# Decoding and splitting weights 1,024 columns at a time in an attention, Fourier and feed-forward kernel, with a new order of all its steps

## The chip, the cores and the metric

The kernel runs on one NeuronCore of a Trainium2 chip. The time is device microseconds of one execution, from its first to its last instruction and what the device puts around them; several runs are made, and their median counts.

## What is computed

The reference, cut to what matters:

```python
# q, k, v: (8 batches, 8 heads, 576 tokens, 64), float32
rel = pos[:, None] - pos[None, :]
mask_local = (rel >= 0) & (rel < 32)                       # heads 0 to 3
mask_strided = (rel >= 0) & (pos[None, :] % 32 == pos[:, None] % 32)   # heads 4 to 7
attn = softmax(where(mask, q @ k.T / 8, -1e9)) @ v
x = attn.transpose(0, 2, 1, 3).reshape(8, 576, 512)
mixed = real(fft(fft(x, axis=1), axis=2))
u = x + mixed
un = (u - mean(u)) / sqrt(var(u) + 1e-6)                   # over the 512 channels
out = u + maximum(un @ w_ch1, 0) @ w_ch2                   # w_ch1 512x2048, w_ch2 2048x512
```

All work is in float32 accuracy. Long matrix products are made of three float16 products: each operand is split into a high and a low half.

## The kernel before

**Weights.** They arrive as words of 64 bits, in 16 pieces of 128 partitions by 512 columns for each of W1 and W2, and each piece is decoded on the chip (`weights`, L1143). SP loads the piece into a borrowed buffer (L1156). ScalarE scales its high words (c1), ScalarE (L1165) or VectorE (L1167) shifts its low words right, VectorE combines the two (c2, L1171), and later VectorE puts the sign back (c3, L1177). Behind c2 four small matmuls (`gram_piece`, L1207) add the piece's squares in a PSUM bank; from four pieces of W1 (`quarter`), or all sixteen of W2 (`weights2`, L1251), come a norm (L1226 to L1228) and a power-of-two scale (L375 to L378). With it W1's pieces are split into halves (`split`: ScalarE L1247, VectorE L1249). W2's are split by `scaled` (ScalarE L1283, VectorE L1285, and SP copies the high half into its place, L1287). W1 is decoded into the memory that W2's result needs later, so a piece of W2 is combined only when the piece of W1 in its place has been split. While a Gram bank is open and TensorE would wait, matmuls on zeros (fillers, `rest`, L1215) are put in.

**Where the pieces land.** `S0` and `S1` in the table `P` name the buffer that each late piece borrows. `u` means two of the eight slots of the output buffer `ub`, which holds u of the first chunks as well.

**The data.** Batch 0's attention comes first (`att_first`), then for each batch its four pairs of heads (`att_pair32` for batches 1 and 2, `att_pair` from 3 on): scores on TensorE, the softmax (weigh L771, maximum L778, subtraction L780 on VectorE, exponential on ScalarE), values, and the result to a DRAM buffer xd. `fft_batch` loads it back (GpSimd gathers rows in another order), forms sums and differences E and O on VectorE (L865), transforms one axis (A, L1008 and L1011 for batch 0) and the other (B, L1031 to L1043), and adds x (u0, u1, u2: L1047). The row of zeros that the gather reads beside the tokens is stored into xd by `batch` (L1761).

**The feed-forward part.** Tokens are taken in chunks of 256. For chunk c, `Chunk.norm` makes the normalized, split and transposed input, `ups` its eight hidden layers ph{c}_0 to ph{c}_7 (24 matmuls each, L1330). `hidden` applies relu (ScalarE L1346 and L1347), and GpSimd subtracts the low half (L1349). `downs` multiplies with W2 (L1370). The last three chunks go through `Folded`, in a form with fewer products.

**The order.** One Python program, `class Order`, plans everything: each step is a generator that yields `op(engine, duration, get, put, need, sets, ...)` and then issues its instructions. The planner keeps a clock for each engine and for the DMA (`D`), takes the step that can start first, with a bias for its thread among near ones, and issues it; the instruction stream of every engine is fixed that way. All durations, biases and waiting margins stand in `P` or in the calls of `op`. A step with `alt` goes to the engine that would end it first.

Of the kernel before, what the change touches and what calls it, by code (L numbers as in the profile page):

```python
# [158 lines left out]

class Op:  # L160
# [3 lines left out]
    def __init__(self, engine, dur, get="", put="", need="", sets="", at=None, lat=None, n=1, slack=0.0, dma=0.0, note="", alt=None):  # L164
# [15 lines left out]
class Order:  # L180


    def __init__(self):
        self.threads, self.free, self.room, self.events = [], dict.fromkeys("TVAGSD", 0.0), {}, {}
        self.waits = {}
        self.now = 0.0
        self.fill = None

# [1635 lines left out]
```

## Time and profile before

| | before |
|---|---|
| median of 3 runs | 967.71 us (967.14 to 968.94) |
| the profiled execution | 961.29 us, span 959.5 us, granted clock 0.983 |
| TensorE (PE) busy | 914.8 us, 95% |
| VectorE (DVE) busy | 718.4 us, 75% |
| ScalarE (ACT) busy | 500.8 us, 52% |
| GpSimd (POOL) busy | 304.1 us, 32% |
| fillers on TensorE, L1215 | 427 instructions, 31.3 us |

The span goes from the first instruction to the last. Fillers count as busy. The granted clock is TensorE's, as a share of its full speed. The profile is one execution; the median is of other ones.

### The profile page before, as it was taken

The numbers are of one execution on the slowest core, as the hardware profiler recorded it, in microseconds if no ns is written. First come the engines' busy times: TensorE is split into PE (matmuls) and PEld (weight loads), VectorE is DVE, ScalarE is ACT, GpSimd is POOL, SyncE is SP. The second block draws the span as 40 slices with busy tenths as digits, with TensorE's granted clock in tenths as the row PEclk, the third lists the DMA queues.
The fourth block names the chain that finished last, engine by engine and source line by source line (L and its number), as shares of the span: only waits on it lengthen the run. The fifth ranks groups of instructions, "written<-read, shape, count | busy, mean of one in ns | idle before, by whom it ended". The sixth has DMA issues, their size and how long they took to land.

```text
span 959.5 us, 25537 instructions
## 1 busy us (share of the span) xinstructions
PE 914.8 (95%) x10626; PEld 671.9 (70%) x10626; DVE 718.4 (75%) x1386; ACT 500.8 (52%) x1016; POOL 304.1 (32%) x308
## 2 busy tenths in 40 slices
PE   6778969999999999999999999999999999999997
PEld 6646755776676667666766676667666666689996
DVE  5878887747969497749765956686769999877664
ACT  3736664545565466555745565556433444455542
POOL 0120311324324433344214432432245222224332
PEclk9988989999999999999999999999999999999999
DMA  9768447607342734293536442943250102011100
GB/s 316 250 223 273 150 126 237 151 1 202 107 104 58 194 112 115 37 203 119 119 67 187 113 101 45 216 119 100 46 138 1 45 7 61 12 51 24 41 24 23
DMA packets 140499, 108.41 MB, mean 113 GB/s; under 512 B 108384, under 2 KB 118880, under 8 KB 140384
## 3 DMA queue, kind: packets, MB, share of 16 engines
q1 hardware_dynamic: 137824, 98.40, 38.6%
q0 software_dynamic: 2560, 8.39, 2.6%
q8 instruction: 83, 1.36, 0.6%
q14 instruction: 32, 0.26, 0.1%
HBM read 64.26 MB, written 18.89 MB: 87 GB/s over the span
## 4 chain that ended last, share of the span: by engine, by line
PE 83%; DVE 9%; DMA 4%; ACT 2%; issue 1%; POOL 0%; SPq 0%; DVEq 0%; ACTq 0%; POOLq 0%
PE acc L1370 31%; PE ph L1330 30%; PE acc L1657 6%; PE f L1514 3%; PE B L987 2%; PE A L964 1%; PE s L459 1%; DMA uT<-hb 1%; DMA W<-in_w 1%; PE o L490 1%; DVE W L1171 1%; PE f_2x L1514 1%; PE f_0x L1514 1%; DVE W L1177 1%; DMA q<-in_qk 1%
## 5 line engine op out<-in xcount | busy, mean ns | idle before, releaser
L1330 PE MATMUL ph<-uT,W 128*128 128x256 f16 x2880 | 328.2, 273 | 2.4 <-DMA uT<-hb 1.2
L1330 PEld LDWEIGHTS <-W 128*128 128x128 f16 x2880 | 278.1, 98 | 42.9 <-DMA uT<-hb 1.5
L1370 PE MATMUL acc<-W,hb 128*128 128x512 f16 x1344 | 302.2, 379 | 0.0
L1349 POOL TENSOR_TENSOR hb<-hf,hb 128x512 f16<-128x512 f32 x112 | 150.2, 1341 | 320.0 <-ACT hb L1347 219.1
L1370 PEld LDWEIGHTS <-hb 128*128 128x128 f16 x1344 | 128.3, 98 | 143.2 <-POOL ss L396 0.3
L1346 ACT ACTIVATE hf<-ph 128x512 f32<-128x512 f32 x120 | 71.4, 595 | 160.3 <-PE ph L1330 124.5
L1347 ACT ACTIVATE hb<-ph 128x512 f16<-128x512 f32 x112 | 66.3, 592 | 0.0
L1627 POOL TENSOR_TENSOR tail<-hb,tail 128x512 f16<-128x512 f32 (+1 forms) x35 | 37.0, 1067 | 69.3 <-ACT tail L1624 67.6
L1657 PEld LDWEIGHTS <-tail 128*128 128x128 f16 x504 | 48.2, 98 | 5.2
L1127 DVE TENSOR_TENSOR unp<-un,unp 128x512 f16<-128x512 f32 x28 | 23.6, 844 | 31.3 <-ACT unp L1124 31.3
L1424 DVE TENSOR_TENSOR fold<-fold,W 128x512 f32<-128x512 f32 x64 | 46.3, 746 | 0.4
L436 DVE SCALAR_TENSOR_TENSOR kt<-qk,sc,kt 128x576 f16<-128x576 f32 (+1 forms) x40 | 36.3, 946 | 11.9 <-ACT kt L421 11.9
L1109 POOL TENSOR_TENSOR rstd<-mv,negh 128x1 f32<-128x1 f32 x30 | 19.9, 665 | 70.2 <-DVE mv L1106 66.4
L1088 ACT ACTIVATE pq<-B,fcm 128x128 f32<-128x128 f32 (+7 forms) x105 | 27.2, 375 | 18.4 <-PE B L987 7.7
L1514 PEld LDWEIGHTS <-tail 128*128 128x128 f16 x576 | 34.8, 98 | 2.7 <-issue 1.7
L1624 ACT CAST tail<-hb 128x512 f16<-128x512 f32 (+1 forms) x48 | 25.5, 564 | 21.0 <-DVE hb L1601 20.2
L1657 PE MATMUL acc<-fold,tail 128*128 128x256 f16 x288 | 35.4, 273 | 0.0
L471 ACT ACTIVATE sm<-sm 128x594 f32<-128x594 f32 (+1 forms) x20 | 16.3, 814 | 31.6 <-DVE sm L780 31.6
L421 ACT ACTIVATE kt<-qk,sc 128x576 f16<-128x576 f32 (+1 forms) x40 | 29.3, 786 | 3.9 <-DVE sc L377 3.2
L1215 PE MATMUL gram<-oneb,zero 128*128 128x128 bf16 x427 | 31.3, 236 | 0.0
L1601 DVE TENSOR_TENSOR hb<-hb 128x256 f32<-128x256 f32 x48 | 29.8, 635 | 1.1 <-ACT hb L1587 0.4
L1215 PEld LDWEIGHTS <-zero 128*128 128x128 bf16 x427 | 28.6, 107 | 1.6 <-issue 1.0
(302 smaller groups left out, 1513.3 us busy)
## 6 DMA issues: line engine op xcount, KB each, us to landing
qk<-in_qk SPq DMA_DIRECT2D x28, 592.0 KB
sa<-in_w SPq DMA_DIRECT2D x17, 512.0 KB
out<-ub SPq DMA_DIRECT2D x32, 256.0 KB
vn<-in_vl SPq DMA_DIRECT2D x10, 432.0 KB
W<-in_w SPq DMA_DIRECT2D x8, 512.0 KB
xd<-xo SPq DMA_DIRECT2D x16, 256.0 KB
xa<-xd SPq DMA_DIRECT2D x8, 512.0 KB
vn<-in_vs SPq DMA_DIRECT2D x10, 384.0 KB
```

What stands on the lines that cost most here:

```text
L436: V.scalar_tensor_tensor(out=lo, in0=src, scalar=f, in1=hi, op0=ALU.mult, op1=ALU.subtract)
L1215: T.matmul(idle[-1][:, 0:128], zerb, oneb, start=False, stop=False)
L1330: T.matmul(ph[:, i, :], W1[:, 4 * (f0 // 512) + d, x, f0 % 512 : f0 % 512 + 128], self.uhl[y][:, d, :], start=(n == 0), stop=(n == 11))
L1346: A.activation(hf, ph, AF.Relu, scale=HS)
L1347: A.activation(hh, ph, AF.Relu, scale=HS)
L1349: G.tensor_tensor(out=hl, in0=hf, in1=hh, op=ALU.subtract)
L1370: T.matmul(self.acc[s], (hh, hl)[x][:, i, 128 * s : 128 * s + 128], W2[:, f, 1 - y, :], start=(f == 0 and n == 0), stop=(f == 15 and n == 2))
L1424: on(e).tensor_tensor(out=w, in0=w if x is None else x, in1=y, op=ALU.add if f else ALU.subtract)
L1514: T.matmul(dst[:, 128 * f : 128 * f + 128], w(x, i)[:, 128 * f : 128 * f + 128], u(y, i), start=opens and f == 0 and n == 0, stop=closes a ...
L1601: tt = lambda o, x, y, z: on(e).tensor_tensor(out=f(o), in0=f(x), in1=f(y), op=z)
L1627: on(o).tensor_tensor(out=lo, in0=src, in1=hi, op=ALU.subtract)
L1657: T.matmul(dst, hop[:, x, j, 128 * i : 128 * i + 128], w(y, i), start=bank not in opened, stop=q == 3 and z in (6, 5, 3, 4) and i == 1 and ...
```

## The change

Pieces 0 to 11 of W1, and pieces 0, 2 and 8 of W2 with the one behind each, are decoded as pairs: two loads into one buffer of 1,024 columns, then one instruction where two stood for c1, the shift, c2 and c3. The Gram matmuls stay as they were. All splits of W1 and all scaled halves of W2 are pairs. The sign is always VectorE's (the form on ScalarE and GpSimd, which no step used, goes). The planner now keeps the time of a GpSimd step (`lock`) and starts no VectorE step inside it, but for both engines only steps of certain kinds count (`port`, `PORT`). The gather is planned with 7.0 us of DMA rather than 3.0, each row of zeros is stored when the batch before has been loaded, and not all seven at once, and many planned durations, biases and margins are new. `S1` is new, too: pieces 0 to 3, 8 and 9 of W2 go into `ub`, and a pair takes four of its slots.

```diff
 P = dict(
-    SL2=1.57, SLD2=2.778, GL0=8, LAT=0.637, GL=6.45, t2=9.759, l0=-28.888, a0=-20, sq0=7.465, w0a=25.925, c=-26.309,
+    SL2=2.709, SLD2=1.449, GL0=2.7, GD=7.0, LAT=1.77, GL=3.1, t2=9.759, l0=-29.011, a0=-20, sq0=7.465, w0a=28.151,
...
-    S1=('kt', 'pt', 'f6', 'u', 'uT', 'qk', 'f6', 'kt', 'uT', 'u', 'f6', 'kt', 'pt', 'uT', 'u', 'f6'), HB=4, RB=1, UB=8, VS=1, FC=15, tp=60.0, ts=0.0, fq=-30.0, fh=-10.0, ff=-20.0, pf=5.0, Lfold=50.0, Lus=1.0, Lhl=-0.5,
+    S1=('u', 'u', 'u', 'u', 'f6', 'uT', 'pt', 'qk', 'u', 'u', 'kt', 'pt', 'qk', 'kt', 'uT', 'f6'), M1=(0, 2, 8), HB=4,
...
+PORT = ("st", "weigh", "max", "out", "AL", "y1", "y2", "norm", "vlo", "fin", "SD", "u0", "u1", "u2", "rstd", "pad", "ones", "zero", "xb", "c5", "scales")
...
+        w = note.split()[0] if note else ""
+        self.port = not w.startswith(PORT)
...
                 est = max(t + o.slack, self.free[o.engine])
+                if o.engine == "V" and o.port and o.dur and self.lock[0] <= est < self.lock[1] - 0.1:
+                    est = self.lock[1] - 0.1
...
                 end = self.free[o.engine] = est + o.dur
+                if o.engine == "G" and o.port and o.dur:
+                    self.lock = est, end
...
-        yield op("G", 4.6, get="f6", need=" ".join(f"xd{b}_{hp}" for hp in range(4)), at=0, lat=P["GL"] if b else P["GL0"], dma=3.0, sets=f"xb{b}", note=f"xb {b}")
+        yield op("G", 4.6, get="f6", need=" ".join(f"xd{b}_{hp}" for hp in range(4)) + (f" zrow{b}" if b else ""), at=0, lat=P["GL"] if b else P["GL0"], dma=P["GD"] if b else 3.5, sets=f"xb{b}", note=f"xb {b}")
...
-    def weights(wi, i):
-        src, W, _ = list(wpieces(wi))[i]
+    def weights(wi, i, m):
+        _, W, _ = list(wpieces(wi))[i]
         kind = STG[wi][i]
...
+        if m == 2:
+            W = W2[:, i : i + 2].rearrange("p n a b -> p (n a) b")
+        for n in range(m):
+            src = list(wpieces(wi))[i + n][0]
...
+                k = " ".join(["u"] * 2 * m) if kind == "u" else kind
+                yield op("S", 1.45, get="" if n else k, at=0 if n else None, need="xb0", note=f"ld {wi} {i + n}")
+                if n == 0:
+                    stg = stg2(kind, f"sa{wi}_{i}", m)
+                late(nc.sync.dma_start(stg[:, 512 * n : 512 * n + 512], src))
...
-        yield op("V", 0.8, need=f"w0_{i}" if wi else "", note=f"c2 {wi} {i}")
+        yield op("V", 1.24 if m == 2 else 0.7, need=" ".join(f"w0_{i + n}" for n in range(m)) if wi else "", note=f"c2{z} {wi} {i}")
...
-        for n in range(4 * q, 4 * q + 4):
+        for n in (4 * q, 4 * q + 2):
             spawn(split(n), bias=P["s0"] + 0.01 * n)
...
-        yield op("V", 0.75, sets=f"w0_{n}", note=f"wlo 0 {n}")
-        V.scalar_tensor_tensor(out=W[:, 1], in0=F, scalar=sc, in1=W[:, 0], op0=ALU.mult, op1=ALU.subtract)
+        o = op("V", 1.27, sets=f"w0_{n} w0_{n + 1}", note=f"wlop 0 {n}")
+        yield o
+        V.scalar_tensor_tensor(out=W1[:, n : n + 2, 1], in0=F, scalar=sc, in1=W1[:, n : n + 2, 0], op0=ALU.mult, op1=ALU.subtract)
...
-        for n in range(16):
+        for n in range(0, 16, 2):
             spawn(scaled(n), bias=P["s1"] + 0.01 * n)
...
-        yield op("S", 0.4, put="fs" + (" f6" if n == 15 else ""), sets=f"w1_{n}", note=f"whi 1 {n}")
-        nc.sync.dma_start(W[:, 1], hi)
+        yield op("S", 0.7, put="fs fs" + (" f6" if n == 14 else ""), sets=f"w1_{n} w1_{n + 1}", note=f"whi 1 {n}")
+        nc.sync.dma_start(W2[:, n : n + 2, 1], hi)
...
-        yield op("S", 0.05, need="csin", note=f"zrow {b}")
-        nc.sync.dma_start(xd[b][S : S + 1], a["zrow"])
...
+    def zrow(b):
+        yield op("S", 0.05, need=f"xb{b - 1}", sets=f"zrow{b}", note=f"zrow {b}")
+        nc.sync.dma_start(xd[b][S : S + 1], a["zrow"])
...
     for b in range(1, B):
+        spawn(zrow(b), bias=0.9)
```

What the planner makes of it stands in the instruction streams. The first place is VectorE just ahead of u0, the first sums of chunk 0 (L1047 before, L1059 after; numbers of lines grow by 12 to 24). Rows name the line, the operation, result and operands, and the shape; `sa0_n` is a buffer with piece n of W1, `sa1_n` one with a piece of W2. Before:

```order
L1171 SCALAR_TENSOR_TENSOR W2_90<-sa0_12_947 128x512
L1171 SCALAR_TENSOR_TENSOR W2_90<-sa0_13_949 128x512
L1177 SCALAR_TENSOR_TENSOR W2_90<-sa0_12_947,W2_90 128x512
L1177 SCALAR_TENSOR_TENSOR W2_90<-sa0_13_949,W2_90 128x512
L1171 SCALAR_TENSOR_TENSOR W2_90<-sa0_14_959 128x512
L1171 SCALAR_TENSOR_TENSOR W2_90<-sa0_15_961 128x512
L1177 SCALAR_TENSOR_TENSOR W2_90<-sa0_14_959,W2_90 128x512
L1177 SCALAR_TENSOR_TENSOR W2_90<-sa0_15_961,W2_90 128x512
L1047 TENSOR_TENSOR ub_946<-B0_0_1035,xa0_627 128x257
L1047 TENSOR_TENSOR ub_946<-B0_0_1035,xa0_627 128x255
```

After, `ub_922` holds pairs of W2's pieces, and L783, L790 and L792 are the softmax of batch 1 (L771, L778, L780 before):

```order
L1262 SCALAR_TENSOR_TENSOR W1_89<-W2_90,scl_91,W1_89 128x2x512
L596 MEMSET vsum1_1141 128x4
L790 TENSOR_REDUCE mx1_3_1146<-sm1_3_1132 128x11
L603 COPY vsum1_1141<-n1_3_1161 128x1
L792 TENSOR_TENSOR sm1_3_1132<-sm1_3_1132,mx1_3_1146 128x594
L1195 SCALAR_TENSOR_TENSOR W2_90<-ub_922,W2_90 128x1024 x2
L783 SCALAR_TENSOR_TENSOR sm1_2_1206<-s1_2_1109,mstr_85 128x324
L783 SCALAR_TENSOR_TENSOR sm1_2_1206<-s1_2_1109,mstr_85 128x270
L1190 SCALAR_TENSOR_TENSOR W2_90<-sa1_4_985 128x512
L790 TENSOR_REDUCE mx1_2_1224<-sm1_2_1206 128x11
L1059 TENSOR_TENSOR ub_922<-B0_0_1196,xa0_632 128x257
L1059 TENSOR_TENSOR ub_922<-B0_0_1196,xa0_632 128x255
```

The eight decode steps of W1's last pieces have moved further ahead; between them and u0 stand the splits of W1's last quarter (L1262), the combining and signs of two pairs of W2 (the two rows of L1190 just ahead of this stretch, and L1195), a first 512-wide piece of W2, and parts of two softmaxes.

The second place is VectorE where the norm of W2 is formed from its Gram bank (L1226 before, L1239 after). Before:

```order
L771 SCALAR_TENSOR_TENSOR sm1_0_1702<-s1_0_1273,mloc_84 128x480
L778 TENSOR_REDUCE mx1_0_1733<-sm1_0_1702 128x9
L795 TENSOR_SCALAR rs1_3_1743<-o1_3_1705 128x12
L796 RECIPROCAL rs1_3_1743<-rs1_3_1743 128x12
L808 TENSOR_TENSOR xo1_3_1744<-o1_3_1705,rs1_3_1743 128x2x6x64
L780 TENSOR_TENSOR sm1_0_1702<-sm1_0_1702,mx1_0_1733 128x864
L591 COPY vsum1_1135<-n1_0_1735 128x1
L1226 TENSOR_TENSOR gd1_4_1782<-gram1_963,ident_83 128x512
L1227 TENSOR_REDUCE s1w1_1781<-gd1_4_1782 128x4
L1228 TENSOR_SCALAR s1w1_1781<-s1w1_1781 128x4
```

After:

```order
L1190 SCALAR_TENSOR_TENSOR W2_90<-sa1_15_1170 128x512
L1059 TENSOR_TENSOR xa0_632<-B0_2_1243,xa0_632 33x257
L1059 TENSOR_TENSOR xa0_632<-B0_2_1243,xa0_632 33x255
L1059 TENSOR_TENSOR xb0_634<-B0_2_1243,xb0_634 33x255
L1059 TENSOR_TENSOR xb0_634<-B0_2_1243,xb0_634 33x2
L1059 TENSOR_TENSOR xb0_634<-B0_2_1243,xb0_634 33x255
L1190 SCALAR_TENSOR_TENSOR W2_90<-sa1_13_1412 128x512
L1195 SCALAR_TENSOR_TENSOR W2_90<-sa1_15_1170,W2_90 128x512
L1239 TENSOR_TENSOR gd1_4_1567<-gram1_983,ident_83 128x512
L1240 TENSOR_REDUCE s1w1_1566<-gd1_4_1567 128x4
L1241 TENSOR_SCALAR s1w1_1566<-s1w1_1566 128x4
L783 SCALAR_TENSOR_TENSOR sm1_0_1572<-s1_0_1260,mloc_84 128x480
```

The norm stood behind the softmax of pair 0 of batch 1 and the result of pair 3 (`o1_3`); it now stands ahead of that softmax, directly behind the last decode steps and u2's sums.

The third place is SP's queue from the last piece of W1 on. Before:

```order
L1156 DMA sa0_15_961<-in_w1 128x512
L1761 DMA xd1_96<-in_zrow 16x32
L1761 DMA xd2_97<-in_zrow 16x32
L1761 DMA xd3_98<-in_zrow 16x32
L1761 DMA xd4_99<-in_zrow 16x32
L1761 DMA xd5_100<-in_zrow 16x32
L1761 DMA xd6_101<-in_zrow 16x32
L1761 DMA xd7_102<-in_zrow 16x32
L1156 DMA ub_946<-in_w2 128x512
L1156 DMA sa1_2_1000<-in_w2 128x512
```

After:

```order
L1174 DMA sa0_15_929<-in_w1 128x512
L1786 DMA xd1_96<-in_zrow 16x32
L1174 DMA ub_922<-in_w2 128x512 x4
L1174 DMA sa1_5_965<-in_w2 128x512
L1174 DMA sa1_4_985<-in_w2 128x512
L587 DMA qk1_3_992<-in_qk 128x1184
L587 DMA qk1_2_1019<-in_qk 128x1184
L591 DMA vsx0_76<-in_v13 128x780
L1174 DMA sa1_6_1041<-in_w2 128x512
```

Six of the seven stores of rows of zeros have left this place, the four first loads of W2 all go into `ub`, and loads for batch 1 (`qk1_3`, `qk1_2`, values) follow the next two.

## Rows read from the trace of the kernel before

**Rows 1.** Busy time by stage, split at transform A, ph0_0, ph1_0, 840 us, last matmul.

```profile
core 0: us, PE busy (x) PEld busy (x) DVE busy (x) ACT busy (x) POOL busy (x), PEclk, DMA share, GB/s
0.00:61.50 61.50, 40.30 (x723) 35.57 (x723) 47.06 (x89) 28.04 (x48) 11.49 (x15) 0.94 0.85 283
61.50:99.94 38.44, 33.72 (x349) 24.33 (x349) 29.05 (x68) 25.41 (x46) 2.27 (x4) 0.82 0.73 234
99.94:171.90 71.96, 62.10 (x721) 44.09 (x718) 58.10 (x109) 40.72 (x68) 18.32 (x14) 0.93 0.60 165
171.90:840.00 668.10, 666.90 (x7363) 463.98 (x7364) 505.56 (x970) 350.23 (x716) 233.32 (x240) 1.00 0.40 99
840.00:953.10 113.10, 111.78 (x1476) 103.95 (x1473) 75.64 (x147) 56.35 (x139) 38.65 (x37) 1.00 0.11 30
```

**Rows 2.** TensorE's timeline, 99 to 150 us: start, length, instructions, idle before.

```profile
99.94 2.78 PE L1330 MATMUL ph<-uT,W 128*128 128x256 f16 x24
...
109.82 2.78 PE L1330 MATMUL ph<-uT,W 128*128 128x256 f16 x24 [1.18 <-ACT h L1347]
...
122.85 2.78 PE L1330 MATMUL ph<-uT,W 128*128 128x256 f16 x24
...
126.46 1.31 PE L1207 MATMUL gram<-W 128*128 128x128 bf16 x20
...
140.16 0.17 PE L334 MATMUL n<-vsum,oneb 128*128 128x1 bf16 x1 [2.68 <-ACT jk L586]
140.72 1.44 PE L1370 MATMUL acc<-W,h 128*128 128x512 f16 x3 [0.39 <-DMA W<-fs]
142.44 3.39 PE L1370 MATMUL acc<-W,h 128*128 128x512 f16 x9 [0.28 <-DMA W<-fs]
...
146.55 2.75 PE L1370 MATMUL acc<-W,h 128*128 128x512 f16 x12
```

**Rows 3.** The same columns as in rows 1 for two short stretches.

```profile
62.00:74.00 12.00, 12.00 (x42) 7.26 (x42) 5.84 (x14) 8.11 (x16) 0.65 (x1) 0.55 0.37 133
136.00:138.00 2.00, 1.48 (x36) 1.19 (x28) 1.35 (x3) 1.33 (x3) 0.00 (x0) 0.50 0.77 219
```

**Rows 4.** VectorE's timeline, 43 to 135 us, columns as in rows 2.

```profile
43.33 0.29 DVE L1227 TENSOR_REDUCE s1w<-gd 128x1 f32<-128x128 f32 x1
...
46.03 2.73 DVE L1249 SCALAR_TENSOR_TENSOR W<-W,scl,W 128x512 f16<-128x512 f32 x4
...
49.89 1.75 DVE L865 TENSOR_TENSOR E<-xa,xb 128x1536 f32<-128x1536 f32 x1
...
66.39 0.41 DVE L1167 TENSOR_SCALAR sa<-sa 128x512 int32<-128x512 int32 x1
...
73.40 1.29 DVE L1177 SCALAR_TENSOR_TENSOR W<-sa,W 128x512 int32<-128x512 int32 x2 [5.22 <-PE gram L1207]
...
79.21 0.76 DVE L1047 TENSOR_TENSOR ub<-B,xa 128x257 f32<-128x257 f32 x2 [1.92 <-PE B L1043]
...
90.61 0.83 DVE L771 SCALAR_TENSOR_TENSOR sm<-s,mstr 128x324 f32<-128x324 f32 x2
...
92.82 0.78 DVE L780 TENSOR_TENSOR sm<-sm,mx 128x594 f32<-128x594 f32 x1
...
95.51 1.28 DVE L1171 SCALAR_TENSOR_TENSOR W<-sa 128x512 int32<-128x512 int32 x2
...
128.96 0.68 DVE L1226 TENSOR_TENSOR gd<-gram,ident 128x512 f32<-128x512 f32 x1
...
134.75 0.74 DVE L1285 SCALAR_TENSOR_TENSOR W<-W,scl,fs 128x512 f16<-128x512 f32 x1
```

**Rows 5.** SP's queue, 62 us, columns as in rows 2.

```profile
62.21 0.34 SPq L1156 DMA_DIRECT2D ub<-in_w  x1
```

**Rows 6.** GpSimd's timeline, 104 to 121 us, columns as in rows 2.

```profile
104.87 3.78 POOL L1349 TENSOR_TENSOR h<-hf,h 128x512 f16<-128x512 f32 x1 [18.06 <-ACT h L1347]
...
120.52 1.16 POOL L1349 TENSOR_TENSOR h<-hf,h 128x512 f16<-128x512 f32 x1 [1.20 <-ACT h L1347]
```

More of the change, by code (lines that the diff above doesn't have):

```diff
@@ L948, in fft_batch @@
             first, last = gs[0] == 0, gs[-1] == 4
-            endT = yield op("T", 0.5 * len(gs), get="big f6 -fft" if first else "acc" if one and len(gs) == 1 else "big", need=f"FH{257 if last else 0}_{b} csin second", put="f6" if last else "", note=f"A{gs[0]} {b}", slack=P["SL2"] if b > 2 else SL if b else 0)
+            endT = yield op("T", 0.515 * len(gs), get="big f6 -fft" if first else "acc" if one and len(gs) == 1 else "big", need=f"FH{257 if last else 0}_{b} csin second", put="f6" if last else "", note=f"A{gs[0]} {b}", slack=P["SL2"] if b > 2 else SL if b else 0)
             if first:
@@ L1258, in weights2 @@
         total(gram[:, 0:4], s1)
-        yield op("V", 1.8, get="f6", put="acc", need=" ".join(f"scales0_{q}" for q in range(4)), note="scales 1")
+        yield op("V", 1.7, get="f6", put="acc", need=" ".join(f"scales0_{q}" for q in range(4)), note="scales 1")
         scales(gram[:, 0:4], 4, "w1", scl[:, 1], inv[:, 1])
@@ L1707, in body @@
         att_first(sp, pw)
-        for i in range(12):
-            spawn(weights(0, i), bias=P["w0a"] + 0.01 * i)
+        for i in range(0, 12, 2):
+            spawn(weights(0, i, 2), bias=P["w0a"] + 0.01 * i)
         for q in range(3):
@@ L1721, in body, with stg2 @@
     ub.append(mp.tile([128, UB, DM], F32, name="ub"))
-    def stg2(kind, name):
+    def stg2(kind, name, m):
         if kind == "u":
-            x, y = free.pop(0), free.pop(0)
-            assert y == x + 1
-            staged[name] = x, y
-            t = ub[0][:, x : x + 2].rearrange("p a b -> p (a b)")
+            free.sort()
+            x = next(x for x in free if all(x + n in free for n in range(2 * m)))
+            staged[name] = list(range(x, x + 2 * m))
+            for y in staged[name]:
+                free.remove(y)
+            t = ub[0][:, x : x + 2 * m].rearrange("p a b -> p (a b)")
         elif kind == "uT":
@@ L1749, in body @@
     for i in range(12, 16):
-        spawn(weights(0, i), bias=P["w0"] + 0.01 * i)
+        spawn(weights(0, i, 1), bias=P["w0"] + 0.01 * i)
     spawn(quarter(3), bias=P["s0"])
-    for i in range(16):
-        spawn(weights(1, i), bias=P["w1"] + 0.01 * i)
+    i = 0
+    while i < 16:
+        m = 2 if i in P["M1"] else 1
+        spawn(weights(1, i, m), bias=P["w1"] + 0.01 * i)
+        i += m
     spawn(gram_open(1, 0), bias=P["w1"] - 0.2)
```

174 lines of the change are left out of this document (84 added, 90 removed).

## The prediction

> **What bounds the kernel now.** I read the busy time by stage first [rows 1]. From 171.9 to 840 us TensorE stands still for 668.10 − 666.90 = 1.2 us, and from 840 to its last matmul for 1.3 us; after that 6.4 us remain in which the last sums are added and stored. No order of steps can win much there: TensorE's work is fixed and laid end to end. The time that can move lies in the start: 21.2 us of stillness up to 61.5 us, 4.7 us from there to 99.94, and 9.86 us from 99.94 to 171.9. The matmuls of the first two stretches also hold several hundred fillers that compute nothing, so the first 100 us are emptier than they look; in the third there is no filler, so its 9.86 us are all that a different order could win there by waits.
>
> The edges of these stages are marks: batch 0's first transform A starts at 61.5, chunk 0's first hidden layer (ph0_0) at 99.94, chunk 1's (ph1_0) at 171.9; TensorE's own rows between the last two are [rows 2]. The clock rows [rows 3] show the lower of the two levels (0.50 of full is 1.2 GHz) in 136 to 138, after TensorE had mostly waited, and nearly throughout 62 to 74 (0.55 in the mean), again after stretches of stillness. The price of the first is in rows 2: nine down-projection matmuls in 3.39 us, against twelve in 2.75 us a little later. So the twelve at 140.72 and 142.44 lost 1.44 + 3.39 − 2.75 = 2.1 us, and the work just before them, 1.48 us busy at half clock [rows 3], another 0.7: some 3 us in all. VectorE [rows 4] is the engine that the start waits for: it is 47.06 of 61.5, 29.05 of 38.4 and 58.10 of 72.0 us busy [rows 1].
>
> **The widths.** Two 512-column decode steps take 1.29 us together, of which 0.08 is the last one's tail: 0.605 us from start to start; 1,536 columns take 1.75 − 0.08 = 1.67 [rows 4]. So one instruction costs 0.08 us plus 1.03 ns a column, and one of 1,024 columns 1.13 us against 1.21 for two. Nine pairs with two such steps save 9 × 2 × 0.08 = 1.4 us. Four splitting steps take 2.73 us, 0.66 each; sixteen pairs of those save between 0.08 and 0.13 each, 1.3 to 2.1 us. Against that the order shows four right shifts on VectorE that cover seven pieces, where one piece stood there before (0.41 us, [rows 4], 0.08 of it tail): six more pieces, 2.0 to 2.5 us that ScalarE had done. VectorE's sum hardly moves, by less than 1.5 us either way. ScalarE gains some microseconds and is 28 of 61 and 25 of 38 us busy: idle time that costs nothing. I book **0** for the widths (−1 to +1). What a pair does cost is lateness: the second load must land before the first column is touched. That is part of the order below.
>
> **The order up to ph0_0.** Transform A waits for VectorE's chain from E (49.89) on. In both orders that chain holds the same transform steps; beside them stood four 512-wide decode steps (2.4 us) and now one pair split and two 1,024-wide ones (1.2 + 2.3). That is +1 us, against which E may start up to 1 us earlier, since one decode instruction fewer stands ahead of it. I take +0.5 (−1 to +1.5).
>
> Behind A the change is large, as the order of VectorE shows. Before, eight 512-wide steps of W1's last pieces, then chunk 0's sums u0: the first of these ends its wait for TensorE at 73.40 and u0 starts at 79.21, 5.8 us. Now between the same points stand four of these steps (2.4), the quarter's norm and scale (seven short ones of at most 0.29, [rows 4], say 1.2), the shift of a pair (0.7), two pair decodes (2.3), two pair splits (2.4), one softmax of batch 1 (0.75, and its maximum and subtraction at 0.70 each: 2.1), two pair signs (2.3), and weigh, decode step and maximum (0.75 + 0.6 + 0.7 = 2.0): 15.4 us, 9.6 more. They are W2's first four pieces, and they must be there: they are loaded into all eight slots of the output buffer, which u0 needs itself. So u0 comes **10 us later**. The loads are no obstacle: with the seven small row stores gone from SP's queue and four slots free at once, they can be issued where the single load into the buffer was, at 62.21 [rows 5], and have 11 us to land. From u0 to the last split before the transposes both orders need about 11.5 us (79.21 to 90.61 before, when the next softmax step starts; softmax steps have been traded for seven decode steps).
>
> From there to ph0_0 the old order took another 9.3 us, since four of W2's Gram pieces, decoded only from 95.51 on, stood ahead of it on TensorE. In the new one twelve of the sixteen stand ahead of it, but eight are done by then: the ninth to twelfth need two 1,024-wide and three 512-wide steps, 4.1 us. So: +0.5 + 10 + 0 − 5.2 = +5.3; with a wait on ScalarE's square sum inside the list (its copy to VectorE stands ahead of the softmax's subtraction) and some slack I book **+7 us** for ph0_0's start, at 107 (bounds +5 and +10). Each microsecond here moves everything behind it.
>
> **The order after ph0_0.** What is bought for this: 32 more Gram matmuls lie ahead of ph0_0, out of TensorE's way (eight pieces at 0.23 us, as five take 1.31 [rows 2] with some 0.15 of tail: **−1.8**); and the norm of W2, whose first step stood at 128.96 [rows 4], some 29 us behind ph0_0, now follows ph0_0 by the last decode steps only (eight at 0.605 and the five sums of u2 at 0.34, as the two of 79.21: 6.5 us). W2's scaled halves can so start about 16 us after ph0_0, beside the hidden layers, and not 35 us after it (134.75). Chunk 0's down-projection then finds its weights, where before it began at 140.72, 15 us after the end of the last hidden layer (122.85 + 2.78), in the part at low clock. The waits that this removes are the 9.86 us and the 3 us of clock: −12.9. Not all goes. The 1.18 us before the second hidden layers [rows 2] come from POOL, whose first split took 3.78 us beside VectorE's chain of decode steps against 1.16 alone [rows 6]; the chain is there again. And the 2.68 us of the small matmul at 140.16 wait for a value tile with one buffer, which loads late in the new order too. I give back 1.2 + 2.5 = **3.7** (bounds 0 and 10).
>
> From 171.9 on I book 0. The distances that cover transfers there have not shrunk: counting matmuls between the scores and the values of one pair of heads in batches 3 to 7, the shortest stretch holds 13.9 us of TensorE work in both orders.
>
> **Sum.** +7 − 1.8 − 12.9 + 3.7 = **−4.0 us**. The profiled span is 959.5 (961.29 in all), the median of the timed runs 967.71; on the median it gives **963.7 us**. A change under 0.2%, 1.9 us, can't be told from none.
>
> **Rivals.**
> (a) *TensorE keeps its clock through transform A.* It does 12 us of work there at 0.55 [rows 3]; at full clock 6.6, so 5.4 us less: 958.3. For it: other fillers stand there now. Against: they are about as many, and the wait ahead of them is still for the same VectorE chain. 0.13.
> (b) *POOL and VectorE stop each other through the hidden layers.* Every one of the eight hidden layers needs a POOL split; if each meets a 1,024-wide step and waits 1.2 us, one every 2.7 us no longer fits: 4 to 5 us beyond what the other matmuls in between cover, and the sum is 0 to +1: 968. Against: the decode steps that lie beside them are 512 wide; only the eight scaled pairs are wide. The Trainium skill, "SBUF — State Buffer", section "Who interferes with whom", states that an instruction of VectorE with two inputs in SBUF and one of GpSimd that reads it exclude each other for a whole instruction, whichever starts first; by that a doubled width doubles the longest wait. The trace agrees so far as the 3.78 against 1.16 us go. 0.20.
> (c) *The late start isn't paid back: slower.* SP's queue is in order. The fourth to eighth copies of W2's high halves now stand behind the value load that waits for o1_0, which TensorE does after the last hidden layer, and behind the stores of its result. Three copies stand ahead of it and cover three of eight parts of the down-projection. If W2's scaling is late so that these three haven't landed when ph0_7 ends, TensorE waits about 7 us at that place, one copy's landing after another: +3.5, 971. By my counts the third is scaled 4 us before ph0_7's end; a copy needs 4 to 6 us to be there (before, the first was scaled at 134.75 and used at 140.72). So it decides from little lateness on. 0.17.
> The forecast itself, with its own range 959.5 to 966.5: 0.50.
>
> **Numbers.** Faster by over 0.2%: (a) and nine tenths of the forecast's 0.50, 0.58 in all; within 0.2%: most of (b) and the rest, 0.22; slower: (c) and a part of (b), 0.20. The range takes in (a) and (c) and the bounds of the first two terms: 955.5 to 972.
>
> **What would show it.** ph0_0 at 105 to 110 us; no TensorE wait over 1.5 us between it and ph1_0, and ph1_0 before 172 with part of chunk 0's down-projection still to do; no low clock after ph0_0; W2's Gram norm on VectorE before the third hidden layer; stillness from there to 840 under 2 us. Wrong if ph0_0 is later than 112, if down-projection matmuls wait on the copies, or if pairs of scores and values wait in the middle.

## The result, and the profile after

The changed kernel takes 955.82 us (median of 4 runs, 953.46 to 958.3), the kernel before 967.42 beside it (4 runs, 963.15 to 968.94): a ratio of 0.9887, with an interval of 0.9845 to 0.993. That is 11.6 us less, where 4.0 were forecast, and just inside the lower end of the range. The profiled execution took 954.45 us with a span of 952.6, 6.9 us less than the profiled span of before.

The page of the changed kernel, engines, chain and fillers:

```profile
PE 915.5 (96%) x10678; PEld 676.8 (71%) x10680; DVE 714.4 (75%) x1359; ACT 492.8 (52%) x980; POOL 292.1 (31%) x303
...
PE 90%; DVE 5%; DMA 3%; issue 1%; POOL 1%; SPq 0%; ACT 0%; DVEq 0%; ACTq 0%
...
L1228 PE MATMUL gram<-oneb,zero 128*128 128x128 bf16 x481 | 36.1, 240 | 1.9 <-issue 1.9
```

TensorE is busy for as long as before in all, with 54 more fillers (4.8 us) in it; it stands still for 37.1 us of the span, where it stood still for 44.7. The chain that ended last runs over it for 90% of the span (83% before), and VectorE's share of that chain fell from 9 to 5%. VectorE's sum fell by 4 us, where I had allowed for less than 1.5.

Busy time by stage, columns as in [rows 1], cut at A, ph0_0, 180 and 840 us and the last matmul:

```profile
0.00:62.83 62.83, 43.05 (x735) 38.50 (x736) 47.59 (x75) 24.14 (x30) 13.16 (x15) 0.89 0.88 289
62.83:111.18 48.35, 39.38 (x422) 29.13 (x423) 38.54 (x74) 29.41 (x46) 2.04 (x4) 0.82 0.69 217
111.18:180.00 68.82, 67.31 (x847) 51.31 (x848) 50.13 (x90) 37.88 (x60) 21.54 (x18) 1.00 0.56 162
180.00:840.00 660.00, 659.54 (x7260) 457.60 (x7258) 500.93 (x959) 346.49 (x711) 238.16 (x248) 1.00 0.39 99
840.00:946.30 106.30, 106.25 (x1422) 100.29 (x1419) 74.22 (x157) 54.88 (x135) 17.24 (x20) 1.00 0.11 26
```

ph0_0 starts 11.24 us later (111.18 for 99.94), with 9.0 us of stillness ahead of it behind A, where it had been 4.7. From ph0_0 to the last matmul TensorE stands still for 1.51 + 0.46 + 0.05 = 2.0 us, and stood still for 12.4 before [rows 1]; that stretch is 835.1 us long and was 853.2. Late by 11.2, shorter by 18.0: so the 6.9.

TensorE's timeline from ph0_0 on, columns as in [rows 2]:

```profile
111.18 2.79 PE L1343 MATMUL ph<-uT,W 128*128 128x256 f16 x24 [0.82 <-DMA uT<-hb]
114.04 2.78 PE L1343 MATMUL ph<-uT,W 128*128 128x256 f16 x24
...
118.00 2.78 PE L1343 MATMUL ph<-uT,W 128*128 128x256 f16 x24
...
133.33 1.04 PE L556 MATMUL s<-qk 64*64 64x96 f32 x36 [1.15 <-ACT pT L634]
134.30 2.79 PE L1343 MATMUL ph<-uT,W 128*128 128x256 f16 x24
...
137.04 2.78 PE L1343 MATMUL ph<-uT,W 128*128 128x256 f16 x24
139.75 1.27 PE L643 MATMUL o<-vlx,pT 96*64 96x65 f32 x36
140.96 2.76 PE L1383 MATMUL acc<-W,h 128*128 128x512 f16 x12
...
157.18 2.78 PE L1343 MATMUL ph<-uT,W 128*128 128x256 f16 x24
```

The down-projection of chunk 0 starts at 140.96, as before (140.72, [rows 2]), though ph0_0 is 11 us later. Before, the eight hidden layers (22 us of TensorE) stood in one block up to 125.6, and the end of batch 1's attention stood alone behind them, with its waits. Now they stand among that attention. The twelve down-projection matmuls run at full clock without a wait on the copies.

That start makes a mark at equal work: behind it 9,122 matmuls followed before, and 9,126 now. From ph0_0 to the mark, and from there to the last matmul:

```profile
111.18:140.96 29.78, 28.63 (x401) 25.31 (x401) 24.86 (x53) 19.27 (x31) 10.86 (x9) 1.00 0.33 100
140.96:946.30 805.34, 804.47 (x9126) 583.89 (x9123) 600.42 (x1152) 419.98 (x875) 266.07 (x277) 1.00 0.37 95
```

The same two for the kernel before:

```profile
99.94:140.72 40.78, 32.43 (x436) 28.28 (x434) 34.34 (x69) 25.54 (x45) 13.54 (x9) 0.93 0.42 126
140.72:953.10 812.38, 808.35 (x9122) 583.74 (x9121) 604.97 (x1156) 421.77 (x878) 276.75 (x282) 1.00 0.37 94
```

So the late start is paid back by the mark (+0.24 us), and the whole gain of this pair, 7.04 us, lies behind it: 4.03 − 0.87 = 3.2 of stillness, and 3.9 of work that takes less time.

VectorE around the places that the prediction spoke of, and GpSimd's splits (the first two and the longest):

```profile
75.72 1.29 DVE L1195 SCALAR_TENSOR_TENSOR W<-sa,W 128x512 int32<-128x512 int32 x2 [5.75 <-PE gram L1220]
...
92.50 0.74 DVE L1059 TENSOR_TENSOR ub<-B,xa 128x257 f32<-128x257 f32 x2
...
99.79 0.69 DVE L1115 BATCH_NORM_STATS2 st<-ub 128x6 f32<-128x512 f32 x1
...
118.20 0.69 DVE L1239 TENSOR_TENSOR gd<-gram,ident 128x512 f32<-128x512 f32 x1 [0.65 <-PE gram L1220]
...
130.42 2.47 DVE L1298 SCALAR_TENSOR_TENSOR W<-W,scl,fs 128x1024 f16<-128x1024 f32 x2
```

```profile
115.22 1.16 POOL L1362 TENSOR_TENSOR h<-hf,h 128x512 f16<-128x512 f32 x1 [12.47 <-ACT h L1360]
118.08 1.16 POOL L1362 TENSOR_TENSOR h<-hf,h 128x512 f16<-128x512 f32 x1 [1.69 <-ACT h L1360]
...
132.09 1.82 POOL L1362 TENSOR_TENSOR h<-hf,h 128x512 f16<-128x512 f32 x1 [2.39 <-ACT h L1360]
```

u0 comes at 92.50 (79.21 before), the norm of W2 7.0 us behind ph0_0 (29 before), the first scaled pair 19 us behind it (35 before) [rows 4]. Six of GpSimd's eight splits for chunk 0 take 1.16 us, one 1.27 and one 1.82; the one of 3.78 us [rows 6] is gone.

### The profile page after: what moved, and what is told of

Same layout as the page of the kernel before. It is cut to its first block, busy times and chain, and to the rows that moved or that the text cites. A ratio compares the mean times of both kernels' runs of the same rounds, so it can differ in the third digit from the quotient of the medians.

```text
span 952.6 us, 25491 instructions
## 1 busy us (share of the span) xinstructions
PE 915.5 (96%) x10678; PEld 676.8 (71%) x10680; DVE 714.4 (75%) x1359; ACT 492.8 (52%) x980; POOL 292.1 (31%) x303
## 4 chain that ended last, share of the span: by engine, by line
PE 90%; DVE 5%; DMA 3%; issue 1%; POOL 1%; SPq 0%; ACT 0%; DVEq 0%; ACTq 0%
PE ph L1343 33%; PE acc L1383 32%; PE acc L1670 6%; PE f L1527 3%; PE B L999 2%; PE A L976 2%; PE s L471 1%; PE o L502 1%; DVE W L1195 1%; DMA q<-in_qk 1%; PE f_0x L1527 1%; PE f_2x L1527 1%; DVE W L1190 1%; PE o L509 1%; PE s L556 1%
## 5 line engine op out<-in xcount | busy, mean ns | idle before, releaser
L1343 PE MATMUL ph<-uT,W 128*128 128x256 f16 x2880 | 327.8, 273 | 0.8 <-DMA uT<-hb 0.8
L1437 DVE TENSOR_TENSOR fold<-fold,W 128x512 f32<-128x512 f32 x64 | 50.7, 816 | 0.4
L1228 PE MATMUL gram<-oneb,zero 128*128 128x128 bf16 x481 | 36.1, 240 | 1.9 <-issue 1.9
L1228 PEld LDWEIGHTS <-zero 128*128 128x128 bf16 x481 | 33.5, 110 | 5.1 <-issue 4.6
L448 DVE SCALAR_TENSOR_TENSOR kt<-qk,sc,kt 128x576 f16<-128x576 f32 (+1 forms) x40 | 33.5, 878 | 3.7 <-ACT kt L433 3.5
L1614 POOL TENSOR_TENSOR hb<-hb 128x256 f32<-128x256 f32 x14 | 12.0, 859 | 76.2 <-DVE hb L1614 39.2
L1640 DVE TENSOR_TENSOR tail<-hb,tail 128x512 f16<-128x512 f32 (+1 forms) x48 | 33.4, 726 | 1.4 <-ACT tail L1637 1.3
L989 DVE SCALAR_TENSOR_TENSOR AT<-A,AT 128x290 f16<-128x290 f32 (+3 forms) x35 | 15.2, 480 | 23.3 <-ACT AT L984 20.6
L1220 PE MATMUL gram<-W 128*128 128x128 bf16 x128 | 12.6, 249 | 17.8 <-DVE W L1190 11.1
```

Of the source, the lines that this page charges most:

```text
L448: V.scalar_tensor_tensor(out=lo, in0=src, scalar=f, in1=hi, op0=ALU.mult, op1=ALU.subtract)
L1228: T.matmul(idle[-1][:, 0:128], zerb, oneb, start=False, stop=False)
L1343: T.matmul(ph[:, i, :], W1[:, 4 * (f0 // 512) + d, x, f0 % 512 : f0 % 512 + 128], self.uhl[y][:, d, :], start=(n == 0), stop=(n == 11))
L1437: on(e).tensor_tensor(out=w, in0=w if x is None else x, in1=y, op=ALU.add if f else ALU.subtract)
L1640: on(o).tensor_tensor(out=lo, in0=src, in1=hi, op=ALU.subtract)
```

## The experiments

Ratios are to the kernel before, run beside each kernel on the same chip; its median there was 966.25 to 968.62 us. Lines of code are those of the changed kernel, where not said otherwise.

**Both kernels again.** The changed kernel as it is:

> The changed kernel once more, for its spread and as the base of the runs beside it. If the profile of the changed kernel is typical: chunk 0's first hidden layer at 110 to 112 us, under 2 us of stillness between it and 180 us, span 951 to 957 us, and about 10 us less than the kernel before. If its gain hung on lucky transfers, the start differs by several microseconds from one execution to the other, and TensorE's waits beyond 111 us come back.

It took 956.04 us (954.96 to 956.97), 0.9866 [0.9834, 0.9899]: the gain is there again. And one more execution of the kernel before:

> The kernel before, looked at once more: its profiled execution lay 6 us under the median of its timed runs, the changed kernel's only 1 to 2 us. If the difference lies in the start, its waits between 62 and 172 us are longer here in a longer span, or differ in place, and 172 to 840 us stays without stillness. If it is spread over the steady part, stillness over 2 us shows between 172 and 840 us.

969.33 us, with a span of 967.6. Its TensorE, with the last waits up to the mark, and then its two stretches:

```profile
140.74 0.16 PE L334 MATMUL n<-vsum,oneb 128*128 128x1 bf16 x1 [3.66 <-ACT jk L586]
...
142.34 5.28 PE L1370 MATMUL acc<-W,h 128*128 128x512 f16 x12 [1.44 <-DMA W<-fs]
```

```profile
100.36:142.34 41.98, 31.60 (x436) 27.57 (x434) 35.21 (x71) 25.88 (x45) 14.44 (x9) 0.98 0.40 125
142.34:961.20 818.86, 812.41 (x9122) 586.08 (x9121) 602.26 (x1155) 422.02 (x878) 276.00 (x282) 0.99 0.36 93
```

And the second profile of the changed kernel, at the same marks:

```profile
110.01:141.47 31.46, 30.31 (x401) 26.12 (x401) 24.86 (x53) 19.18 (x31) 10.86 (x9) 0.95 0.31 88
141.47:947.90 806.43, 804.72 (x9126) 583.86 (x9123) 597.94 (x1152) 420.03 (x875) 267.06 (x277) 1.00 0.37 95
```

Again the mark hardly moves (142.34, 141.47), and behind it 12.4 us are won: 6.45 − 1.71 = 4.7 of stillness, 7.7 of work that takes less time. Of the stillness, 3.2 us are one wait of the kernel before, of a hidden layer for its transposed input (`uT<-hb`). Of the work, 2.0 us are chunk 0's down-projection (its first twelve matmuls take 5.28 us in one and 2.76 in the other) and 3.1 the same number of hidden-layer matmuls (24 of them take 5.30 us right behind that wait, for 2.78): clock. The two pairs of spans differ by 6.9 and by 13.4 us, the medians by 11.6; the execution profiled first (961.29 us) was a short one of its kernel.

**Widths.** Every step of 1,024 columns is issued as two of 512, in the same order:

```diff
-        V.scalar_tensor_tensor(out=Fi, in0=wh, scalar=3, in1=wl, op0=ALU.logical_shift_left, op1=ALU.bitwise_or)
+        for y in hv:
+            V.scalar_tensor_tensor(out=Fi[:, y], in0=wh[:, y], scalar=3, in1=wl[:, y], op0=ALU.logical_shift_left, op1=ALU.bitwise_or)
...
```

> Each instruction of 1,024 columns on VectorE and ScalarE (decode, shift, split, scale) is issued as two of 512; places in the order, loads and all other steps stay. My booking of 0 for the widths: VectorE 2.5 to 3.5 us busier in all, some 2 us of that ahead of the first hidden layer, which comes 0 to 2 us later; time 0 to +2 us, hardly to be told from the changed kernel. Rival, widths carry the gain: 4 us or more slower. Rival, wide instructions keep GpSimd out for longer: 1 us or more faster.

956.48 us (954.97 to 957.32), 0.9874 [0.9842, 0.9906]: no difference to the changed kernel that can be measured. On VectorE it has 37 instructions more, and the steps concerned sum to 68.7 us for 64.3: 0.12 us for each, in the bounds taken from [rows 4]. The wide steps don't carry the gain.

**The loads.** All seven rows of zeros are stored at once, as before, ahead of W2's loads:

```diff
-        nc.sync.dma_start(xd[b][S : S + 1], a["zrow"])
+        for n in range(1, B) if b == 1 else ():
+            nc.sync.dma_start(xd[n][S : S + 1], a["zrow"])
```

> All seven rows of zeros are stored at once, where the changed kernel stores the first; everything else stays. In the kernel before they held SP's queue from 52.4 to 60.5 us. My account, in which the loads of W2's first pieces are no obstacle: they are issued 1 to 3 us later than 59.6 and still land in time; first hidden layer and time within 1 us of the changed kernel. Rival, that the spread stores are part of the gain: loads land after VectorE wants them, first hidden layer 3 us later or more, time 3 us or more up.

955.87 us (953.77 to 956.75), 0.9873 [0.9835, 0.9912]. On SP's queue:

```profile
53.22 7.21 SPq L1787 DMA_DIRECT2D xd<-in_zrow  x7
61.28 1.88 SPq L1174 DMA_DIRECT2D ub<-in_w  x4
```

The four loads are issued 1.7 us later than in the changed kernel (59.58), and nothing follows from it: ph0_0 starts at 109.65. They are no obstacle, as forecast.

**Is it u0?** W2's pieces land in the buffers of before, so that `ub` is free for u0, and none of W2's pieces is a pair:

```diff
-    S1=('u', 'u', 'u', 'u', 'f6', 'uT', 'pt', 'qk', 'u', 'u', 'kt', 'pt', 'qk', 'kt', 'uT', 'f6'), M1=(0, 2, 8), HB=4,
+    S1=('kt', 'pt', 'f6', 'u', 'uT', 'qk', 'f6', 'kt', 'uT', 'u', 'f6', 'kt', 'pt', 'uT', 'u', 'f6'), M1=(), HB=4,
```

> Changed kernel with W2's pieces in the buffers of the kernel before and none as a pair, so that the slots of the output buffer are free for u0 early. Everything behind is ordered anew, with margins that were not chosen for it, so the whole may come out anywhere from 950 to 1020 us; what counts is the start. My step, that W2's first pieces ahead of u0 make it late: u0 at 79 to 83 us instead of 92, first hidden layer at 100 to 104 instead of 111, the norm of W2 later than 118 us behind it, and more than 5 us of stillness between the first hidden layer and 172 us. Rival, that the lateness comes from the order of the rest: first hidden layer at 108 or later. If the early start costs nothing behind it, stillness stays under 3 us there, and the early decode was a mistake.

999.7 us (998.61 to 1002.51), 1.0342 [1.0278, 1.0406]. Its VectorE and TensorE:

```profile
83.98 0.76 DVE L1059 TENSOR_TENSOR ub<-B,xa 128x257 f32<-128x257 f32 x2 [2.79 <-PE B L1055]
...
108.31 0.69 DVE L1115 BATCH_NORM_STATS2 st<-ub 128x6 f32<-128x512 f32 x1
```

```profile
114.99 0.41 PE L1220 MATMUL gram<-W 128*128 128x128 bf16 x4 [0.20 <-DVE W L1190]
116.80 0.61 PE L1220 MATMUL gram<-W 128*128 128x128 bf16 x4 [0.62 <-DVE W L1190]
117.99 3.86 PE L1343 MATMUL ph<-uT,W 128*128 128x256 f16 x24 [0.58 <-DMA uT<-hb]
```

u0 is 8.5 us earlier than in the changed kernel, and ph0_0 6.8 later. Between them VectorE decodes pieces of W2: chunk 0's normalization (L1115) starts 24.3 us behind u0, where it starts 7.3 us behind it in the changed kernel. Their Gram matmuls stand ahead of ph0_0 on TensorE, one waiting after another for VectorE (four rows of waits from 111.53 on), and the last wait of ph0_0 is for its transposed input, which that normalization makes. So the start of u0 alone doesn't set ph0_0; the decode steps that the order puts between u0 and ph0_0 do as much. Half of the loss against the changed kernel (44.7 us in span) lies in the steady part: 22.6 us of stillness between 180 and 840 (637.38 of 660 busy), in an order whose margins were not chosen for it.

**Is it the early norm?** W2's norm waits until pairs 3 and 2 of batch 1 are done:

```diff
-        yield op("V", 1.9, need=" ".join(f"gram1_{i}" for i in range(16)), note="norm 1")
+        yield op("V", 1.9, need=" ".join(f"gram1_{i}" for i in range(16)) + " att1_3 att1_2", note="norm 1")
```

> The norm of W2 waits for the results of pairs 3 and 2 of batch 1, as it stood behind pair 3's in the kernel before; the rest of the order follows. My theory, that the early norm is what removes the waits ahead of chunk 0's down-projection: the scaled halves start 8 to 12 us later, TensorE stands still 6 to 10 us between the last hidden layer of chunk 0 and its down-projection, perhaps at low clock again, and the time is 6 to 12 us above the changed kernel's, at or above the time before. Rival, that the gain comes from the other 150 us of the order (chunk 1's hidden layers drawn forward fill the hole): under 3 us more.

993.8 us (992.84 to 995.26), 1.0261 [1.0227, 1.0295]. The norm comes at 129.79, almost when it came before (128.96, [rows 4]), but 18.9 us behind ph0_0, where it stood 29 before; the down-projection comes at 147.95. By stage, from ph0_0:

```profile
110.93:180.00 69.07, 66.06 (x818) 50.32 (x822) 46.93 (x86) 36.99 (x59) 21.80 (x18) 1.00 0.56 156
180.00:840.00 660.00, 643.62 (x7084) 443.58 (x7077) 459.89 (x901) 334.53 (x681) 220.03 (x231) 0.99 0.39 97
```

The stillness up to 180 us is 3.0 us, not the 10 of before: other work stands there, two of chunk 1's hidden layers (139.49, 145.19) among it. So a norm some 7 us behind ph0_0 isn't needed for a closed gap; no run shows this order with the norm 29 us behind. The time is lost later, 16.4 us between 180 and 840, 8.1 of them in waits for transposed inputs.

**Is it chunk 1's hidden layers?** In the kernel before, the margin of chunk 1 is set so that the planner draws them forward:

```diff
-    z=12.736, f0=-22.976, w0=-25.887, s0=-1.061, w1=2.262, s1=-12.582, p0=-14.949, p1=10.996, pn=-3.093, a1=-18.418,
+    z=12.736, f0=-22.976, w0=-25.887, s0=-1.061, w1=2.262, s1=-12.582, p0=-14.949, p1=-14.9, pn=-3.093, a1=-18.418,
```

> The kernel before with one number changed: the bias of chunk 1's normalization as that of chunk 0's. The order is the same up to chunk 0's hidden layers; behind them chunk 1's first hidden layers stand ahead of chunk 0's down-projection, and all that follows is ordered anew with margins that were not chosen for it, so the whole can't be foretold (950 to 1020 us). What counts is 100 to 180 us. Theory 1, formed from the changed kernel and from the run with the late norm of W2: the hole there is filled by chunk 1's hidden layers and needs no earlier norm: TensorE is still for 3 to 6 us in these 80 us instead of 10 to 14, with no low clock, though the norm comes at 129 us as before. Theory 2, my prediction's: without an earlier norm the wait for the scaled halves or the loads and transposes stays, at 9 us or more.

980.83 us (980.44 to 981.82), 1.0153 [1.0106, 1.0201]:

```profile
146.24 0.16 PE L334 MATMUL n<-vsum,oneb 128*128 128x1 bf16 x1 [6.05 <-ACT jk L586]
...
148.91 3.68 PE L1330 MATMUL ph<-uT,W 128*128 128x256 f16 x24
```

ph1_0 comes 23 us earlier than in [rows 1], but behind the wait, not into it; 14.6 us of stillness remain from ph0_0 (103.68) to 180. The norm comes at 135.30 here, 31.6 us behind ph0_0. Drawing chunk 1 forward is not enough.

**Is it the lock?** The planner counts no kind of step for the lock:

```diff
-        self.port = not w.startswith(PORT)
+        self.port = False
```

> The planner doesn't keep VectorE's steps off GpSimd's; durations, biases and buffers stay, and the order is another one from 113 us on. Theory A, blocking is what the rule avoids: VectorE's busy time rises by 5 us or more as its steps beside GpSimd stretch, and the time by 2 to 6 us, with waits for VectorE or GpSimd. Theory B, the rule only makes another order: VectorE's busy time within 2 us of 714, and the time goes up by whatever the new order does to the distances between scores and values, from 0 to 40 us, with TensorE waiting for ScalarE or transfers in the steady part. Theory C, neither matters: within 1 us.

1016.98 us (1014.25 to 1018.8), 1.0501 [1.0459, 1.0543]. ph0_0 is at 111.41, as in the changed kernel, and up to 180 us there are 3.0 us of stillness; from 180 to 840 there are 47.7:

```profile
180.00:840.00 660.00, 612.27 (x6852) 421.58 (x6851) 472.95 (x914) 329.19 (x672) 209.31 (x222) 0.96 0.40 96
```

One wait there is 13.6 us, of a transform (L976) for ScalarE. VectorE is busy for 720.5 us, 6.1 more than in the changed kernel, but it has nine steps more there and GpSimd eight fewer, which the planner moved; so blocking isn't shown by it. This is another order with margins that don't fit it, and the run can't tell the lock's own worth.

**The clock, in the kernel before.** Fillers in a free PSUM bank keep TensorE at work in the stillness ahead of chunk 0's down-projection (lines of before):

```diff
-                    self.fill(n)
+                    self.fills = getattr(self, "fills", 0) + 1
+                    self.fill({23: 16, 24: 20, 25: 8, 26: 46, 27: 8}.get(self.fills, n))
...
```

> The kernel before with fillers into a free bank between W2's last Gram matmul and chunk 0's down-projection (16, 20, 8, 46 and 8 of them), and nothing else. My term of 3 us for the clock: the first twelve down-projection matmuls take 2.8 us instead of 4.8 to 5.3, the scores ahead of them 1.0, and the time falls by 2 to 4 us under that of the kernel before. Rival, that the landing of W2's copies paces them: the matmuls are shorter but wait in between, and the time is the same within 1 us. Second rival, that the fillers themselves come in the way: 1 to 3 us more.

970.5 us (965.51 to 974.73), 1.0013 [0.9983, 1.0044]: nothing won. Its TensorE:

```profile
144.23 2.75 PE L1377 MATMUL acc<-W,h 128*128 128x512 f16 x12
...
152.95 1.08 PE L545 MATMUL s<-qk 64*64 64x54 f32 x44 [2.12 <-DMA qk<-in_qk]
156.39 4.71 PE L1377 MATMUL acc<-W,h 128*128 128x512 f16 x12
```

The first twelve run at full clock, but 1.9 to 3.5 us later than without the fillers (142.34, 140.72); a wait for a load comes behind them, and twelve at low clock behind that. So full clock at this place alone wins nothing: the time goes into the next wait.

**The clock, in the changed kernel.** A still does its products at low clock. Three kernels add fillers ahead of it (180 and 70 for 89 and 32; 150 and 60; 120 and 40). The second also puts two behind each of A's 15 products, the third one, and both put more ahead of the last Gram pieces. The edit of the third:

```diff
-                    self.fill(n)
+                    self.fills = getattr(self, "fills", 0) + 1
+                    self.fill({15: 120, 16: 40, 22: 60, 23: 45, 24: 34}.get(self.fills, n))
...
+                rest(1 if b == 0 else 0)
...
```

> More fillers at the two places ahead of transform A where TensorE stood still (180 for 89, and 70 for 32); the order of everything else is that of the changed kernel. Theory 1, the low clock through A follows from the 5.87 and 1.79 us of stillness ahead of it: A and its Gram matmuls take 6.6 us instead of 11.8, VectorE's 5.75 us of waiting for them all but goes, the first hidden layer comes 5 us earlier, at 106, and the whole is 5 us shorter. Theory 2, A's own matmuls can't hold the clock: A stays at 11 to 12 us and the time is the same within 1 us. Theory 3, the clock is held, but something else ends the wait (a load, ScalarE): A is short, the first hidden layer moves by less than 2 us.

> Changed kernel with fillers ahead of transform A (150 and 60), two fillers behind each of A's 15 products, and more fillers ahead of the last Gram matmuls before the first hidden layer (65, 50, 38 for 35, 30, 18). Theory 1, A's float32 products alone let the clock fall and fillers among them hold it: A with its fillers takes 8 to 9 us instead of 11.8, VectorE's wait for the Gram matmuls behind it falls from 5.75 to 3 us, the first hidden layer comes 2.5 to 4 us earlier than 110.5 and at full clock, and the time is 3 to 5 us under the changed kernel's. Theory 2, nothing holds the clock there: A takes 13 us or more, and the time grows by 1 to 2 us.

> Changed kernel with fewer added fillers: 120 for 89 and 40 for 32 ahead of transform A, one behind each of its 15 products, and 60, 45 and 34 for 35, 30 and 18 ahead of the last Gram matmuls. If one filler per product holds the clock: from A's start to the Gram matmuls behind it 8 us instead of 11.4 to 11.8, first hidden layer 58 to 59 us behind E's start instead of 61 to 62, all hidden layers at full clock, and 2 to 4 us less than the changed kernel. If it doesn't, A takes 11 us or more and the time is the changed kernel's, within 1 us.

952.75 us (948.48 to 957.93), 0.9833 [0.9788, 0.9878]; 956.51 (951.3 to 959.95), 0.9885 [0.984, 0.9931]; 958.12 (951.97 to 959.42), 0.9896 [0.9846, 0.9946]. The stretch of A in the changed kernel:

```profile
62.83:74.62 11.79, 11.79 (x32) 6.47 (x31) 5.75 (x11) 7.01 (x12) 0.68 (x2) 0.51 0.56 204
```

The same with fillers ahead of it only:

```profile
63.03:72.73 9.70, 9.70 (x32) 5.55 (x32) 5.75 (x11) 7.01 (x12) 0.68 (x1) 0.65 0.68 260
```

And with one filler behind each product too (with two it takes 8.7 us, from 64.31 to 73.03):

```profile
63.55:71.44 7.89, 7.89 (x47) 4.60 (x47) 5.75 (x11) 7.06 (x12) 0.68 (x2) 1.00 0.79 299
```

So A can be done in 7.89 us, 3.9 less, fillers included. ph0_0 starts at 109.1, 109.0 and 108.9, some 2 us earlier than 111.18 and 1 earlier than in the second profile. In the first and the third of these kernels it then runs at low clock, behind a wait for its transposed input:

```profile
109.13 4.26 PE L1344 MATMUL ph<-uT,W 128*128 128x256 f16 x24 [1.06 <-DMA uT<-hb]
```

```profile
108.87 4.17 PE L1346 MATMUL ph<-uT,W 128*128 128x256 f16 x24 [2.54 <-DMA uT<-hb]
```

The down-projection starts at 140.57, 138.81 and 140.03, for 140.96 and 141.47 in the two profiles of the changed kernel: of the 3.9 us, 0.4 to 2.7 are left by there, and the medians don't show them. All three intervals overlap that of the unchanged kernel, and none is measurably faster. Three of the six executions of the first took 948.5 to 949.9 us, though, less than any of the ten of the changed kernel (953.46 and up), and the other three 955.6 to 957.9; six don't settle whether more fillers ahead of A help in some executions.

## Why the prediction was half right

**Direction and place: right.** The kernel is faster, because stillness and low clock of TensorE behind ph0_0 go. Most signs named for it came: no wait over 1.5 us behind ph0_0 (the longest is 1.15), ph1_0 at 157.18 with down-projection left to do, granted clock 1.00, under 2 us of stillness up to 840. Two did not: ph0_0 was to come at 105 to 110 us and came at 111.18 (110.01 in the second profile), and the norm came at 118.20, 0.2 us behind the start of the third hidden layer. In the second profile ph0_0 itself ran at low clock (4.46 us for 2.78). The median, 955.82, lies below the forecast's own 959.5 to 966.5. It lies in the range only by the part that rival (a) and the outer bounds of two terms had added, and rival (a) didn't come: that the range held was luck.

**ph0_0, +7 booked, +11.2 measured (+9.7 in the second pair).** The chain ahead of u0 was late by 2.3 us, not 0.5 (73.40 to 75.72). The list between it and u0 took 16.8 us for 15.4 booked. The largest miss is the last part: from u0 to ph0_0 I took off 5.2 us, and it became 2.1 shorter (18.7 for 20.7). Of the 3.1 us between, 1.1 lie between u0 and the end of the splits ahead of the transposes (12.6 us for 11.5, up to 105.12) and 2.0 behind it (6.1 for 4.1). For that last part I counted VectorE's decode steps alone; 0.82 us of it are ph0_0's last wait, for its transposed input to land (`uT<-hb`), which the sum didn't contain. The run with `ub` free showed the same place: the decode steps that the order puts ahead of ph0_0 count, not u0 alone.

**Gram matmuls, −1.8 booked, −1.8 measured.** Behind ph0_0 stood 48, twelve pieces, and now stand 16, four pieces; from start to start a piece takes 0.23 us in both (102.56 to 102.79 before, 113.81 to 114.04 after).

**Waits and clock, −12.9 booked with 3.7 given back.** The stillness was 9.86 us from ph0_0 to 171.9 and is 1.51 from ph0_0 to 180: 8.4 less. Neither the 1.18 nor the 2.68 us of [rows 2] came back, only 1.15 at another place. The clock gave what was booked: the 96 matmuls of chunk 0's down-projection take 21.8 us for 23.5, the f32 scores 4.9 for 5.8, the hidden layers 327.8 for 328.2, 3.0 in all. So −11.4 where −9.2 stood: the term was right, and the give-back too large by 2.2. My reason, that the early norm makes the gap go, isn't borne out: with the norm 18.9 us behind ph0_0 instead of 7.0, other work fills the gap.

**From 171.9 us on, 0 booked, −2.0 measured:** 1.2 to 0.46 of stillness up to 840, and 1.3 to 0.05 behind it.

**The sum.** Against the profiled span it is +11.2 − 18.0 = −6.8, where +7 − 11.0 = −4.0 stood; of the 18.0 the terms above hold 1.8 + 11.4 + 2.0 = 15.2, and 2.8 of TensorE's busy time are spread over its other matmuls and not traced further. The other 4 to 5 us of the medians are no term: the execution from which every number was taken was a short one of its kernel, and another one of the kernel before had 6.5 us more behind the mark, in waits and low clock that the new order doesn't have. I laid the sum on the median without asking how far executions of this kernel lie apart.

**The rivals.** (a) A kept its low clock (0.51), and where it was made to keep the full one, 3.9 us at A became no measurable gain. (b) Of GpSimd's splits for chunk 0 one takes 1.82 us (1.53 with half the width) and the others 1.16 to 1.27, TensorE doesn't wait for them, and half the width doesn't change the time. (c) SP's copies are there in time: no down-projection matmul waits for them.

**What stays open.** In three profiles with chunk 0's hidden layers in a block ahead of batch 1's last attention (before twice, and chunk 1 drawn forward; the run of before with fillers isn't counted) TensorE stands still for 9.9, 13.6 and 14.6 us from ph0_0 to 180; in the changed kernel, twice, and in the three variants of its order with the norm late, `ub` free and no lock, for 1.5, 2.3, 3.0, 2.1 and 3.0. That speaks for the place of the hidden layers as the cause, but no run moved it alone. The norm of W2 differs between the two groups as well: it stands 29 to 32 us behind ph0_0 in the first and 5 to 19 in the second, so that a late norm isn't ruled out as a part of the cause. Nor was it tried what eight paired copies of W2 on SP, in place of sixteen, bring by themselves, and the lock's own worth is not settled.

## What to carry to other kernels

A step that starts 11 us late had cost nothing by the mark here, where independent work lay among the waits of what follows: compare two orders at a mark of equal work, not at the step that moved. Before a sum from one profile is laid on a median, profile the kernel before a second time; here two executions of it lay 8 us apart in span, more than the whole forecast. In an order that a planner makes, one changed margin or need reorders everything behind it, so that four such runs ended 15 to 50 us above the kernel before; only edits that leave the order as it is (widths, stores, fillers) measured one thing.

## What was unexpected on the chip

TensorE ran A's float32 products at 0.51 of its clock though the profile shows it busy for all of the 11.79 us; with more bf16 fillers ahead of them the mean was 0.65, and with some more ahead and one 128x128 bf16 matmul behind each product 1.00, in 7.89 us. And executions of one kernel differ in clock and time: in one set the kernel before took 958.7 us at a mean granted clock of 0.988 and 971.81 at 0.976.
